# Attention's second product in two chains of 256 query columns instead of one of 512

## The chip, the core and the metric

The kernel runs on one core of one Trainium2 chip. The metric is the device time of one execution in microseconds (us). Before the change the median of three runs is 1011.43 us (1008.32 to 1012.51). TensorE multiplies matrices, VectorE (DVE) and ScalarE (ACT) work on tiles elementwise, GpSimd (POOL) does elementwise work on SBUF alone, and SyncE (SP) issues the DMAs of this kernel, one after the other from one queue.

## The reference

Four batches (B = 4) of 12288 queries with C = 128 channels attend to 768 pooled keys each; keys and values are the same matrix. What comes out goes through a gated convolution of five taps along the sequence.

```python
kv_pool = kv.reshape(B, H // r, r, W // r, r, C).mean(axis=(2, 4))   # r = 4
k = v = kv_pool.reshape(B, -1, C) @ w_sr                             # 768 x 128
s = (q @ k.transpose(0, 2, 1)) / np.sqrt(C)
a = np.exp(s - s.max(-1, keepdims=True))
a /= a.sum(-1, keepdims=True) + 1e-09
x = a @ v                                                            # "AV"
gate = sigmoid(sum(conv_w[k] * xp[:, k:k + S] for k in range(5)))    # xp: x, 4 zeros ahead
return (gate * (x @ w_val)) @ w_out
```

## The kernel before, in words

**Groups and tiles.** Queries are taken in groups of 512 (GQ), 24 per batch, 96 in all. A group has four tiles of 128 queries (NT = 4). Everything is kept with the channels or the queries on the partitions, and the output is transposed back on the host.

**A tile.** `score` (L335) makes the 128 × 768 scores in PSUM with six f32r matmuls of 384 columns: queries and keys are each split into a high and a low part, and three of the four products are summed. `row_max` (L349, DVE) takes the negated maximum, `expo` (L354, ACT) the exponential in place with its sum `z`, `norm` (L359, DVE) the reciprocal `r`. `p_hi` (L373, ACT) writes the normalized probabilities as f16 into `hl`, and `p_lo` (L376, DVE) what f16 left over into the other half of the same `hl` tile. One `hl` tile holds two tiles of queries (0 and 1, or 2 and 3 of a group), high and low. When the second of the two is done, `p_lo` issues one DMA transposition from SP (L383), which writes the pair, now with the keys on the partitions, into its half of the group's `pt` tile. `hl` has four buffers and so has `pt`; ACT may write an `hl` buffer again once its transposition has landed.

**AV.** `av_range` (L389) multiplies the values with `pt`. The 768 keys are six chunks of 128 (NCH = 6); for each chunk there are three products (high values × high probabilities, low × high, high × low), listed in `AV_ORDER`, 18 in all. Each is a weight load of 128 × 128 f16 values and a matmul over the 512 query columns of the group, and all 18 are summed in one PSUM tile `av`, which has one buffer. `av_slice` (L395) issues a stretch of the 18.

**The gated part.** `g_x` (L406, ACT) takes `av` out of PSUM into `x`. POOL makes the convolution of two groups at a time out of eight instructions of 1024 columns (`conv_step`, L428). ACT takes the tanh of it, `g_val` (L467) multiplies `x` with `w_val` on TensorE, `g_h` (L471, DVE) joins the two, `g_out` (L478) multiplies with `w_out`, and `g_evac` (L488, ACT) writes the output tile. Four groups are stored with one DMA.

**The order of the work.** Nothing schedules: the order is written by hand. The loop of L583 goes over all 384 tiles, `t`. In step `t` the scores of tile `t + 1` are issued first, then (for the tile before) `p_lo` with its DMA, a load of queries for four groups if it is due, `expo` of tile `t`, then a part of an older group's AV, then the rest. With a lag of one step, `mj` = 0, 1, 2, 3 counts the steps of a group, and `AV_CUTS` gives the parts of the AV of the group two back: at `mj` = 0 the products 0 to 2, at 1 the products 3 to 8 in two halves (something else may stand between them), at 2 the products 9 to 11, at 3 the products 12 to 17. At `mj` = 0, `g_out` of an older group stands on TensorE between the scores and AV; at `mj` = 2, `g_val` stands behind AV. The setup of the next batch's keys (loads of `kv` tiles at 8 of 24 groups until the last batch is loaded, sums on DVE, projections and transposes on TensorE) is spread over the steps.

**SP's queue** holds, in the order of the program: the transpositions, two per group; a load of queries and a store of output per four groups; the `kv` loads. 

**The end.** The last groups' gated parts are written out from L666. The last-but-one group's 18 products stand there in one piece (L681); the last group's AV is already made in two chains of 256 columns, in two banks (L702 to L706). Temporaries of these groups come from the pool `work`, under the names `th2` (two buffers) and `hh` (one).

Of the kernel before, what the change touches and what calls it, by code (L numbers as in the profile page):

```python
# [6 lines left out]
F32 = mybir.dt.float32  # L7
# [8 lines left out]
R = 4  # L16
P = 128
GQ = 512
NT = GQ // P
# [8 lines left out]
def attn_moe_kernel(ctx, tc, qT, kvT, w_sr, w_moe, outT):  # L28
# [3 lines left out]
    B, C, N = qT.shape  # L32
    PC = kvT.shape[4] // R
    NK, RR = PIECES * PC, R * R
    NCH = NK // P
# [2 lines left out]
    NW = w_moe.shape[1]  # L38
    TAPS = NW - 2 * C
    HALO = TAPS - 1  # L40
    AV_CUTS = (0, 3, 9, 12, 18)
    assert 3 * NCH == AV_CUTS[-1]
    scale = 1.0 / float(C) ** 0.5

    const = ctx.enter_context(tc.tile_pool(name="const", bufs=1))
    kvp = ctx.enter_context(tc.tile_pool(name="kvp", bufs=3))
    keys = ctx.enter_context(tc.tile_pool(name="keys", bufs=2))
    io = ctx.enter_context(tc.tile_pool(name="io", bufs=2))
    hlp = ctx.enter_context(tc.tile_pool(name="hlp", bufs=4))
    ptp = ctx.enter_context(tc.tile_pool(name="ptp", bufs=4))  # L50
    work = ctx.enter_context(tc.tile_pool(name="work", bufs=2))
    xp = ctx.enter_context(tc.tile_pool(name="xp", bufs=3))
# [6 lines left out]
    def misc():  # L59
        return ps_m.tile([P, GQ], F32, name="m")  # L60
# [248 lines left out]
    def quad_tile(g):  # L309
        g.quad = io.tile([C, 4, GQ], F32, name="q")  # L310
        for k in range(4):
            at(g.i + k).q = g.quad[:, k]

    def load_q(g, c0=0, c1=4 * GQ):
        nc.sync.dma_start(out=g.quad.rearrange("c i x -> c (i x)")[:, c0:c1],
                          in_=qT[g.b, :, g.t0 + c0:g.t0 + c1])
# [18 lines left out]
    def score(g, j, early=False):  # L335
        sl = slice(j * P, (j + 1) * P)
        kh, kl = g.st["kh"], g.st["kl"]
        s = bank_pair()
        passes = ((g.qh, kh), (g.qh, kl), (g.ql, kh))
        order = [(i, h) for i in range(3) for h in range(2)]  # L340
        if early:
            order.sort(key=lambda p: p[1])
        for i, h in order:
            a, k = passes[i]
            nc.tensor.matmul(s[:, h, :HALF], a[:, sl], k[:, h * HALF:(h + 1) * HALF],  # L345
                             start=(i == 0), stop=(i == 2))
        g.s[j] = s[:, :, :HALF]
# [6 lines left out]
    def expo(g, j):  # L354
        g.z[j] = small.tile([P, 1], F32, name="z")
        nc.scalar.activation(out=g.s[j], in_=g.s[j], func=AF.Exp, bias=g.nm.pop(j),  # L356
                             accum_out=g.z[j])
# [18 lines left out]
    def p_lo(g, j):  # L376

        nc.vector.scalar_tensor_tensor(out=part(g, j, 1), in0=g.s.pop(j), scalar=g.r.pop(j),  # L378
                                       in1=part(g, j, 0), op0=ALU.mult, op1=ALU.subtract)
        if j % 2:  # L380
            if g.pt is None:
                g.pt = ptp.tile([P, NT, 2 * NCH, P], F16, name="pt")
            nc.sync.dma_start_transpose(  # L383
                out=g.pt[:, j - 1:j + 1].rearrange("p j k q -> p (j k) q"),
                in_=g.hl.rearrange("p j a k -> p (j a k)"))

    AV_ORDER = [(v, k, a) for k in range(NCH) for v, a in (("vh", 0), ("vl", 0), ("vh", 1))]

    def av_range(g, out, lo, hi, j0=0, j1=NT):  # L389
        for i in range(lo, hi):  # L390
            v, k, a = AV_ORDER[i]
            nc.tensor.matmul(out, g.st[v][:, k * P:(k + 1) * P], g.pt[:, j0:j1, a * NCH + k],  # L392
                             start=(i == 0), stop=(i == len(AV_ORDER) - 1))

    def av_slice(g, lo, hi):  # L395
        if lo == 0:
            g.av = ps_av.tile([C, GQ], F32, name="av")
        av_range(g, g.av, lo, hi)

    def new_x(g):  # L400
        if g.i % 2 == 0:
            g.two = xp.tile([C, HALO + 2 * GQ], F32, name="x")
            at(g.i + 1).two = g.two
        g.x = g.two[:, g.i % 2 * GQ:g.i % 2 * GQ + HALO + GQ]

    def g_x(g, av, c0=0, c1=GQ):  # L406
        nc.scalar.activation(out=g.x[:, HALO + c0:HALO + c1], in_=av, func=AF.Copy,  # L407
                             scale=g.st["down"])
# [62 lines left out]
    def g_h(th, m, name="h", h=None):  # L471
        if h is None:
            h = work.tile([C, GQ], F32, name=name, bufs=2 if name == "h" else 1)
        nc.vector.scalar_tensor_tensor(out=h, in0=th, scalar=1.0, in1=m,  # L474
                                       op0=ALU.add, op1=ALU.mult)
        return h

    def g_out(h, m):  # L478
        nc.tensor.matmul(m, wout, h, start=True, stop=True)  # L479
        return m  # L480
# [22 lines left out]
    for b in range(B):  # L503
        for i in range(NG):
            g = Group()
# [6 lines left out]
    def at(i):  # L512
        return groups[i] if 0 <= i < G else None
# [31 lines left out]
    for n, i in enumerate(order):  # L545
# [3 lines left out]
        h = 2 * n // PIECES  # L549
# [3 lines left out]
        if n in ends:  # L553
            project(st, h, m, c0 - h * HALF, (n + 1) * PC - h * HALF)
            c0 = (n + 1) * PC
# [22 lines left out]
    def drip():  # L578
        if trickle:
            trickle.pop(0)()  # L580

    row_max(at(0), 0)
    for t in range(NT * G + LAG):  # L583
        gi, j = divmod(t, NT)
        cur, prev, nxt = (at(u // NT) for u in (t, t - 1, t + 1))
        load = j == 0 and gi % 4 == 0 and at(gi + 4)
        gi, mj = divmod(t - LAG, NT)
        avg, xg, vg, og = (at(gi - d) for d in (2, 3, 6, 7))
        cg = at(gi - 4 - gi % 2)

        if nxt:
            score(nxt, (j + 1) % NT)
        if og and mj == 0:
            og.m = g_out(og.h, misc())
        if prev and t <= NT * G:
            p_lo(prev, (j - 1) % NT)
        if load:
            quad_tile(load)
            load_q(load)
        if cur:  # L600
            expo(cur, j)
        if xg and mj == 0:
            new_x(xg)
            g_x(xg, xg.av)
        if og and mj == 1:
            out_tile(og)
            g_evac(og, og.m)
        evac = None
        if avg:
            av_slice(avg, AV_CUTS[mj], AV_CUTS[mj] + 3)  # L610
        if gi == 1 and mj > 0:
            evac = values(st, mj - 1)
        elif mj == 1 and gi > 0:
            evac = setup_product(gi)
        if avg:
            av_slice(avg, AV_CUTS[mj] + 3, AV_CUTS[mj + 1])
        if vg and mj == 2:
            vg.m = g_val(vg, misc())
            vg.th = g_tanh(vg.gate)
        if cg:  # L620
            if mj == 0 and cg.i == gi - 4:
                halo(cg, at(cg.i - 2), nc.gpsimd)
            conv_step(cg, gi % 2 * 4 + mj)
        if mj == 3 and gi >= 0 and at(gi + 2):
            g_qh(at(gi + 2))
        if t == 0:
            row_max(cur, 1)
        if cur:
            norm(cur, j)
            p_hi(cur, j)  # L630
        if nxt and t:
            row_max(nxt, (j + 1) % NT)
        if evac:
            evac()
        if mj == 1 and gi in highs:
            b, q = highs[gi]
            keys_high(states[b], q)
        if vg and mj == 3:
            vg.h = g_h(vg.th, vg.m)
        if gi >= 0 and mj < 3:  # L640
            setup_vector(gi, mj)
        if mj == 1 and gi in loads:
            b, p = loads[gi]
            load_kv(b, states[b], 2 * p)
        if (gi, mj) in halved:
            presum(states[1], halved[gi, mj])
        if gi < 3 and (gi, mj) > (1, 1) and (gi, mj) < (2, 1):
            n = 4 * gi + mj - 6
            values_high(st, n)
            values_low(st, n)  # L650
        if mj == 3 and gi in highs:
            b, q = highs[gi]
            keys_low(states[b], q)
        if mj == 3 and gi > 1 and gi % NG in (NG - 1, 0, 1) and (gi + 1) // NG < B:
            for f in (values_high, values_low):
                f(states[(gi + 1) // NG], (gi + 1) % NG)
        for _ in range(6 if t == 0 else 1):
            drip()
        if mj == 3 and gi >= 0 and at(gi + 2):
            g_ql(at(gi + 2))  # L660
        if mj == 3 and gi in scales:
            scale_values(states[scales[gi]], 0)
        if og and mj == 2 and og.i % 4 == 3:
            store_last(og, 4)

    n1, n2, n3, n4, n5, n6, n7 = groups[:-8:-1]  # L666
    half = GQ // 2
    two = lambda: (lambda p: (p[:, 0], p[:, 1]))(bank_pair())
    one = lambda: bank_pair()[:, 0]

    def gate_tile(name):
        return work.tile([C, GQ], F32, name=name)

    def av_bank():
        return ps_av.tile([C, GQ], F32, name="av")
# [2 lines left out]
    g_x(n3, n3.av)  # L678
    a0, a1 = two()
    n6.m, n5.m = g_val(n6, a0), g_val(n5, a1)  # L680
    av_slice(n2, 0, 18)  # L681
    n6.th, n5.th = g_tanh(n6.gate), g_tanh(n5.gate, gate_tile("th2"))
    halo(n4, n6, nc.scalar)
    acc4 = one()
# [1 line left out]
    n7.m = g_out(n7.h, misc())  # L686
    gate3 = conv_pool(n3)
    n6.h = g_h(n6.th, n6.m)
    n5.h = g_h(n5.th, n5.m, "hh")
    conv_rest(n4, acc4)  # L690
    new_x(n2)
    g_x(n2, n2.av)
# [30 lines left out]
    n2.m = g_val(n2, misc())  # L723
    n1.m = g_val(n1, one())
    n4.m = g_out(n4.h, n4.m)
    n3.h = g_h(n3.th, n3.m, "hh")
    n1.th = gate_tile("th2")
    for c in (0, half):
        g_tanh(acc1[:, c:c + half], n1.th[:, c:c + half])
# [2 lines left out]
    h = work.tile([C, 2 * GQ], F32, name="tap1", bufs=1)  # L732
# [40 lines left out]
```

## Time and profile before

| | |
|---|---|
| median of three runs | 1011.43 us |
| the profiled execution | 1011.84 us, its span 1010.0 us |
| TensorE clock granted | 0.996 of full speed |
| matmuls of AV (L392) in the profile | 1152 with the high values, 576 with the low ones |
| weight loads in the profile, all lines | 4523 |
| DMA transpositions | 192, from issue to landing 3.3 / 6.4 / 9.9 us (least, median, most) |

How to read it. The profile is of one execution. A row of the timeline is "start, duration, engine, line, operation, output <- inputs, shapes, count"; neighbouring equal instructions are joined. PE is TensorE's matmuls and PEld its weight loads, which run beside the matmuls; a matmul's recorded duration is its way through the array, and as matmuls overlap, what one costs is the step from its start to the next one's. "SPq" rows are instructions of SP's queue; their duration is the time for which SP was occupied by one. "idle <- X" or "A <- X: us, times, longest" is the idle time of an engine before an instruction, put down to what ended last; "issue" means that the profile shows nothing that was waited for. The chain is followed back from the last instruction, at each step to what released it.

### The profile page before, as it was taken

To read this page: it belongs to the slowest core of one execution; us is meant where nothing else is said; L and a number is where in the kernel's file an instruction comes from. 1 tells how busy PE (TensorE), PEld (TensorE's weight loads), DVE (VectorE), ACT (ScalarE), POOL (GpSimd) and SP (SyncE) were. 2 spreads that over 40 slices of the span, in tenths; PEclk is the share of its full clock that TensorE was granted. 3 is DMA by queue.
4 is the path that set the end of the run, shared out by engine and by line. 5 is a ranking of instruction groups with operands and counts; after the bars stand their busy time and mean duration, and the time that the engine had idled before them with its cause. 6 is when DMAs were issued, how large, how long until landed. Compare 5 with 4: busy or idle time off the path is not lost.

```text
span 1010.0 us, 14940 instructions
## 1 busy us (share of the span) xinstructions
PE 970.9 (96%) x4523; PEld 647.7 (64%) x4523; DVE 931.1 (92%) x1842; ACT 913.8 (90%) x1599; POOL 868.9 (86%) x653
## 2 busy tenths in 40 slices
PE   3789999999999999999999999999999999999998
PEld 3556666666666666666666666666666666666664
DVE  5899999999999999999999999999999999999996
ACT  1789999999999999989999999898999999999995
POOL 1659989888998889898899998889899989988993
PEclk9899999999999999999999999999999999999999
DMA  9799999999999999999999999999999999999995
GB/s 344 180 197 217 227 225 240 249 222 232 240 236 224 218 244 238 236 227 230 250 220 229 230 253 237 211 247 244 218 222 213 223 206 202 236 207 203 204 195 144
DMA packets 613087, 227.81 MB, mean 226 GB/s; under 512 B 597520, under 2 KB 598160, under 8 KB 607248
## 3 DMA queue, kind: packets, MB, share of 16 engines
q1 hardware_dynamic: 613008, 226.86, 107.2%
q8 instruction: 37, 0.61, 0.2%
q14 instruction: 42, 0.34, 0.1%
HBM read 50.66 MB, written 25.17 MB: 75 GB/s over the span
## 4 chain that ended last, share of the span: by engine, by line
PE 79%; DVE 6%; DMA 6%; ACT 2%; issue 1%; ACTq 0%; DVEq 0%
PE s L345 33%; PE av L392 32%; PE m L468 7%; PE m L479 6%; DMA pt<-hl 6%; DVE hl L378 3%; DVE nm L351 1%; ACT hl L374 1%; DVE h L474 1%; DVE s L447 0%; ACT s L356 0%; DVE r L365 0%; DVE pool L118 0%; PE m L210 0%; ACT o L489 0%
## 5 line engine op out<-in xcount | busy, mean ns | idle before, releaser
L426 POOL TENSOR_TENSOR acc<-acc,tap 128x1024 f32<-128x1024 f32 x184 | 437.2, 2376 | 7.2
L392 PE MATMUL av<-pt,vh 128*128 128x512 f16 (+1 forms) x1152 | 408.9, 380 | 12.1 <-DMA pt<-hl 5.2
L378 DVE SCALAR_TENSOR_TENSOR hl<-s,r,hl 128x768 f16<-128x768 f32 x384 | 388.8, 1012 | 25.5 <-ACT hl L374 21.5
L374 ACT ACTIVATE hl<-s,r 128x768 f16<-128x768 f32 x384 | 346.1, 901 | 45.7 <-DVE r L365 30.3
L351 DVE TENSOR_REDUCE nm<-s 128x1 f32<-128x768 f32 x384 | 362.8, 945 | 18.5 <-PE s L345 15.2
L356 ACT ACTIVATE s<-s,nm 128x768 f32<-128x768 f32 x384 | 335.5, 874 | 17.9 <-DVE nm L351 15.2
L345 PE MATMUL s<-kh,qh 128*128 128x384 f32 x768 | 288.2, 456 | 6.3 <-DVE z L363 5.6
L392 PEld LDWEIGHTS <-vh 128*128 128x128 f16 x1164 | 113.2, 97 | 171.1 <-issue 79.7
L392 PE MATMUL av<-pt,vl 128*128 128x512 f16 (+1 forms) x576 | 217.6, 378 | 0.0
L345 PEld LDWEIGHTS s<-kh,qh 128*128 128x128 f32 x768 | 145.7, 191 | 93.5 <-issue 47.3
L421 POOL TENSOR_SCALAR tap<-x,wm 128x1024 f32<-128x1024 f32 x184 | 204.5, 1126 | 0.0
L345 PE MATMUL s<-kh,ql 128*128 128x384 f32 x768 | 197.0, 337 | 0.0
L345 PE MATMUL s<-kl,qh 128*128 128x384 f32 x768 | 196.8, 337 | 0.0
L326 POOL TENSOR_TENSOR ql<-q,qh 128x512 fp32r<-128x512 f32 (+1 forms) x97 | 123.0, 1268 | 42.4 <-ACT qh L321 42.2
L345 PEld LDWEIGHTS s<-kl,qh 128*128 128x128 f32 x768 | 140.1, 189 | 0.0
L345 PEld LDWEIGHTS s<-kh,ql 128*128 128x128 f32 x768 | 139.7, 189 | 0.0
L421 POOL TENSOR_SCALAR acc<-x,wm 128x1024 f32<-128x1024 f32 x46 | 51.6, 1122 | 50.8 <-ACT x L407 50.2
L479 PE MATMUL m<-h,wm 128*128 128x512 f32 x182 | 93.0, 592 | 0.0
L468 PE MATMUL m<-x,wm 128*128 128x512 f32 x182 | 92.9, 592 | 0.0
L392 PEld LDWEIGHTS <-vl 128*128 128x128 f16 x582 | 57.5, 99 | 51.2 <-issue 29.8
L365 DVE RECIPROCAL r<-z 128x1 f32<-128x1 f32 x384 | 62.9, 164 | 13.1
L356 ACT ACTIVATION_READ_ACCUMULATOR s<-s,nm 128x1 f32 x384 | 74.6, 194 | 0.0
(84 smaller groups left out, 661.0 us busy)
## 6 DMA issues: line engine op xcount, KB each, us to landing
q<-in_q SPq DMA_DIRECT2D x23, 1024.0 KB, 6.0
out<-o SPq DMA_DIRECT2D x22, 1024.0 KB, 4.9
kvt<-in_kv SPq DMA_DIRECT2D x24, 768.0 KB, 5.3
pt<-in_kv SPq DMA_DIRECT2D x16, 384.0 KB, 7.9
pt<-hl SPq DMA_TRANSPOSE x192, 6.2
out<-o SPq DMA_DIRECT2D x3, 512.0 KB, 2.6
q<-in_q SPq DMA_DIRECT2D x1, 512.0 KB, 6.4
acc<-in_w_moe SPq DMA_DIRECT2D x1, 261.0 KB, 6.1
```

The lines of the kernel that those rows point to most:

```text
L326: nc.gpsimd.tensor_tensor(out=g.ql[:, c0:c1], in0=g.q[:, c0:c1], in1=g.qh[:, c0:c1].bitcast(F32), op=ALU.subtract)
L345: nc.tensor.matmul(s[:, h, :HALF], a[:, sl], k[:, h * HALF:(h + 1) * HALF], start=(i == 0), stop=(i == 2))
L351: nc.vector.tensor_reduce(out=nm, in_=g.s[j], axis=AX.XY, op=ALU.max, negate=True)
L356: nc.scalar.activation(out=g.s[j], in_=g.s[j], func=AF.Exp, bias=g.nm.pop(j), accum_out=g.z[j])
L365: nc.vector.reciprocal(out=g.r[j], in_=z)
L374: nc.scalar.activation(out=part(g, j, 0), in_=g.s[j], func=AF.Copy, scale=g.r[j])
L378: nc.vector.scalar_tensor_tensor(out=part(g, j, 1), in0=g.s.pop(j), scalar=g.r.pop(j), in1=part(g, j, 0), op0=ALU.mult, op1=ALU.subtract)
L392: nc.tensor.matmul(out, g.st[v][:, k * P:(k + 1) * P], g.pt[:, j0:j1, a * NCH + k], start=(i == 0), stop=(i == len(AV_ORDER) - 1))
L421: nc.gpsimd.tensor_scalar(out=t, in0=g.two[:, k:k + 2 * GQ], scalar1=cwt[:, k:k + 1], scalar2=1.0, op0=ALU.mult, op1=ALU.mult)
L426: nc.gpsimd.tensor_tensor(out=g.acc, in0=g.acc, in1=t, op=ALU.add)
L468: nc.tensor.matmul(m, wval, g.x[:, HALO + c0:HALO + c1], start=True, stop=True)
L479: nc.tensor.matmul(m, wout, h, start=True, stop=True)
```

## The change

The AV of a group becomes two chains of 18 products of 256 columns. The first sums over tiles 0 and 1 into the left half of the `av` tile, the second over tiles 2 and 3 into the right half. `AV_CUTS` is doubled, so that at `mj` = 0 and 1 the first chain is issued (6 and 12 products) and at `mj` = 2 and 3 the second (6 and 12). The pool of `hl` tiles has five buffers. To make room for it, `th2` and `hh` of the last groups are no longer taken from `work`: two of the `kv` buffers, which nothing loads any more at that point, are cut into six tiles of 512 columns (`spare`). Nothing else is different: the loop, the loads, the transpositions and the numbers of all other buffers stay.

```diff
-    AV_CUTS = (0, 3, 9, 12, 18)
-    assert 3 * NCH == AV_CUTS[-1]
+    AV_CUTS = (0, 6, 18, 24, 36)
+    assert 6 * NCH == AV_CUTS[-1]
...
-    hlp = ctx.enter_context(tc.tile_pool(name="hlp", bufs=4))
+    hlp = ctx.enter_context(tc.tile_pool(name="hlp", bufs=5))
...
     def av_slice(g, lo, hi):
+
         if lo == 0:
             g.av = ps_av.tile([C, GQ], F32, name="av")
-        av_range(g, g.av, lo, hi)
+        for n in range(2):
+            c0, n0 = n * GQ // 2, n * len(AV_ORDER)
+            av_range(g, g.av[:, c0:c0 + GQ // 2], max(lo - n0, 0), min(hi - n0, len(AV_ORDER)),
+                     n * NT // 2, (n + 1) * NT // 2)
...
         if avg:
-            av_slice(avg, AV_CUTS[mj], AV_CUTS[mj] + 3)
+            av_slice(avg, AV_CUTS[mj], AV_CUTS[mj] + 6)
...
         if avg:
-            av_slice(avg, AV_CUTS[mj] + 3, AV_CUTS[mj + 1])
+            av_slice(avg, AV_CUTS[mj] + 6, AV_CUTS[mj + 1])
...
+    idle = [kvp.tile([C, 2, R, PC * R], F32, name="kvt").rearrange("c n r x -> c (n r x)")
+            for _ in range(2)]
+    spare = [t[:, c:c + GQ] for t in idle for c in range(0, 3 * GQ, GQ)]
+
     def gate_tile(name):
-        return work.tile([C, GQ], F32, name=name)
+        return spare.pop() if name == "th2" else work.tile([C, GQ], F32, name=name)
...
-    av_slice(n2, 0, 18)
+    av_slice(n2, 0, AV_CUTS[-1])
...
-    n5.h = g_h(n5.th, n5.m, "hh")
+    n5.h = g_h(n5.th, n5.m, h=spare.pop())
...
-    n3.h = g_h(n3.th, n3.m, "hh")
+    n3.h = g_h(n3.th, n3.m, h=spare.pop())
```

## The prediction

> **What bounds the kernel now.** I read the page first, for the busy shares and the chain that ended last.
>
> ```profile
> PE 970.9 (96%) x4523; PEld 647.7 (64%) x4523; DVE 931.1 (92%) x1842; ACT 913.8 (90%) x1599; POOL 868.9 (86%) x653
> PE 79%; DVE 6%; DMA 6%; ACT 2%; issue 1%; ACTq 0%; DVEq 0%
> ```
>
> TensorE is busy nearly all the time and holds 79% of the chain; the transpositions (DMA pt<-hl) hold 6%. Where the two meet is seen by stage, in the busy times of three stretches:
>
> ```profile
> core 0: us, PE busy (x) PEld busy (x) DVE busy (x) ACT busy (x) POOL busy (x), PEclk, DMA share, GB/s
> 100.00:230.00 130.00, 130.00 (x612) 86.95 (x611) 125.73 (x256) 124.05 (x217) 117.74 (x86) 1.00 1.12 231
> 230.00:690.00 460.00, 452.04 (x2115) 300.05 (x2112) 434.56 (x879) 428.92 (x747) 415.73 (x306) 1.00 1.12 234
> 690.00:980.00 290.00, 290.00 (x1363) 193.91 (x1362) 267.48 (x512) 275.40 (x476) 262.84 (x189) 1.00 1.06 213
> ```
>
> From 100 to 230 us and from 690 to 980 us TensorE never idles. All its idle time in the steady part, 460 − 452 = 8.0 us, lies between 230 and 690 us. The answer on the AV line says for what it waited there (us, times):
>
> ```profile
>   DMA pt<-hl: 8.8, 11
> ```
>
> So eleven times the weight load in front of a group's AV waited for a transposition, 8.8 us in all. Two of the waits show on the chain, each with the transposition from its issue to its landing:
>
> ```profile
> 445.21 5.71 DMA pt<-hl
> 450.91 0.14 issue
> ...
> 675.24 9.43 DMA pt<-hl
> 684.67 0.14 issue
> 684.81 0.81 PE av L392 x3
> ```
>
> In both cases AV starts 0.14 us after the landing. What a group costs where nothing waits is read from the chain at 800 us, from one product with wm to the next of its kind:
>
> ```profile
> 798.81 0.86 PE m L468 x2
> 799.66 1.04 PE s L345 x6
> 800.71 1.31 PE av L392 x6
> ...
> 803.92 0.65 PE av L392 x3
> ...
> 807.98 0.66 PE av L392 x3
> 808.64 0.86 PE m L468 x2
> ```
>
> 808.64 − 798.81 = 9.83 us for a group. The group's first AV slice is at 803.92 and its third at 807.98, 4.06 us later.
>
> Why the transpositions are late is a matter of SP's queue. Near the last wait (first the DVE instruction that completes a tile pair, then SP):
>
> ```profile
> 674.42 1.01 DVE L378 SCALAR_TENSOR_TENSOR hl<-s,r,hl 128x768 f16<-128x768 f32 x1
> ...
> 680.76 0.53 SPq L315 DMA_DIRECT2D q<-in_q  x1
> 681.40 6.44 SPq L383 DMA_TRANSPOSE pt<-hl  x1
> ...
> 834.01 1.02 DVE L378 SCALAR_TENSOR_TENSOR hl<-s,r,hl 128x768 f16<-128x768 f32 x1 [0.17 <-ACT hl L374]
> ...
> 835.10 5.44 SPq L383 DMA_TRANSPOSE pt<-hl  x1
> ```
>
> The pair finished at 675.43 is issued only at 681.40, 6.0 us late; at 835 us, where no kv tiles are loaded any more, the delay is 0.07 us. And SP has no gap at the end of the loaded stretch:
>
> ```profile
> 681.40 21.77 SPq L383 DMA_TRANSPOSE pt<-hl  x5
> 703.27 0.53 SPq L495 DMA_DIRECT2D out<-o  x1
> 703.89 14.08 SPq L383 DMA_TRANSPOSE pt<-hl  x3
> 718.07 0.53 SPq L315 DMA_DIRECT2D q<-in_q  x1
> 718.70 21.30 SPq L383 DMA_TRANSPOSE pt<-hl  x5
> ```
>
> Each row begins where the one before it ends. So in that stretch the waits of TensorE have a second cause behind them: a queue that serves as fast as it can.
>
> **The change part by part.** The sum is made against the profiled execution's own 1011.84 us (span 1010.0 and 1.84 around it), 0.41 above the median of 1011.43.
>
> *Two chains of 256 columns.* The trace has both forms, at its end:
>
> ```profile
> 988.28 0.38 PE L392 MATMUL av<-pt,vh 128*128 128x512 f16 x1
> ...
> 991.95 0.38 PE L392 MATMUL av<-pt,vh 128*128 128x512 f16 x1
> ...
> 994.74 0.27 PE L392 MATMUL av<-pt,vh 128*128 128x256 f16 x1
> ...
> 998.56 0.27 PE L392 MATMUL m<-pt,vh 128*128 128x256 f16 x1
> 998.67 0.59 PE L468 MATMUL s<-x,wm 128*128 128x512 f32 x1
> ```
>
> From the first to the last of 18 wide ones are 17 steps in 3.67 us, 0.2159 each; from the first to the last of 36 narrow ones 35 steps in 3.82 us, 0.1091 each. Per group 36 × 0.1091 − 18 × 0.2159 = 3.928 − 3.886 = 0.042 us more. TensorE sets the pace from about 100 to 980 us, 880 / 9.83 = 89 groups: +3.7 us. The bounds: 0, if a narrow one took exactly half; +6.6 us, if it took the 0.110 that an 18-step chain of 1.98 us gives (36 × 0.110 − 3.886 = 0.074 per group). I take 3.7, since it is the same instruction, merely elsewhere.
>
> [...]
>
> *36 more weight loads per group.* Their rows, and those of the scores:
>
> ```profile
> L392 PEld LDWEIGHTS <-vh 128*128 128x128 f16 x1164 | 113.2, 97 | 171.1 <-issue 79.7 <-DMA pt<-hl 3.6
> L345 PEld LDWEIGHTS s<-kh,qh 128*128 128x128 f32 x768 | 145.7, 191 | 93.5 <-issue 47.3 <-PE s L345 2.9 <-DVE z L363 1.6
> ```
>
> An f16 load of 97 ns fits beside a matmul of 109 ns, which the 0.1091 already shows. The f32 load that follows a chain has 191 ns in the record and now only 109 ns of cover instead of 216. The one place where the trace has this, 998.56 to 998.67, has the f32 product starting 0.11 us after the last narrow one: nothing is left uncovered. I take 0; the other end is 0.191 − 0.109 = 0.082 us, four times a group, +29 us (a rival below).
>
> *The second half is asked for 4.06 us later.* The order of TensorE's queue at the start of one group's AV; the names behind "waits" are counters, DMAHW those of transfers. Before:
>
> ```order
> L479 MATMUL m<-h,wm 128x512 [waits DVE_49]
> L392 LDWEIGHTS vh [waits DMAHW5_49,DMAHW3_49]
> L392 MATMUL av<-pt,vh 128x512 [waits Activation_49]
> L392 LDWEIGHTS vl
> L392 MATMUL av<-pt,vl 128x512
> ```
>
> Now, the first chain and, some 40 rows on, the start of the second:
>
> ```order
> L483 MATMUL m<-h,wm 128x512 [waits DVE_49]
> L392 LDWEIGHTS vh [waits DMAHW0_49]
> L392 MATMUL av<-pt,vh 128x256 [waits Activation_49]
> ...
> L345 MATMUL s<-kh,ql 128x384
> L392 LDWEIGHTS vh
> L392 MATMUL av<-pt,vh 128x256 [waits DMAHW2_49]
> L392 LDWEIGHTS vl
> ```
>
> The first load waits for one transposition instead of two, and the wait for the pair of tiles 2 and 3 has moved behind two score tiles. Behind the moved wait stand that chain and the next scores, for which DVE and ACT wait. The old waits, by the view of who waited for whom (us, times, longest):
>
> ```profile
> PE av L392 <- DMA pt<-hl: 5.2, 7, 1.6
> PEld L392 <- DMA pt<-hl: 3.6, 4, 1.6
> ```
>
> None is over 1.6 us, so 4.06 covers each of them taken alone: −8.8 us.
>
> *The fifth hl buffer.* ACT waited for the transposition of an old pair:
>
> ```profile
> ACT hl L374 <- DMA pt<-hl: 2.1, 3, 1.1
> ```
>
> With the queue allowed to run later this would grow; a fifth buffer gives one pair, 4.9 us, more. I count 0 on the path: the waits fell where TensorE waited too.
>
> *The tail.* DVE, ACT and SP keep their order, the temporaries only take other memory, and the 36 narrow matmuls there cost 0.04 us. 0.
>
> **The sum, by two accounts.** By TensorE's: 1011.84 − 8.8 + 3.7 = 1006.7. But the queue has an account of its own. Its services don't get shorter, and while it never runs empty it can't land a pair sooner. The first pair of the last late group was issued at 681.40, and the answer on that one transposition and the load that begins the group's AV read:
>
> ```profile
> DMA to landing us min/median/max: 8.5/8.5/8.5
> ...
> 694.21 0.10 PEld L392 LDWEIGHTS <-vh 128*128 128x128 f16 x1 [0.24 <-issue]
> ```
>
> It lands at 689.9, and with the 0.14 us seen above AV can start at 690.0 instead of 694.21: 4.2 us sooner and no more, however few the waits. Where the queue begins to lag, somewhere between 100 us and the first idle time after 230, TensorE comes up to 13 groups × 0.042 = 0.5 us later than before; I take 0.2: 4.0. After that TensorE is alone again and pays 0.042 on (980 − 694) / 9.83 = 29 groups, +1.2. So 1011.84 − 4.0 + 1.2 = 1009.0, and 0.41 less on the scale of the median: 1008.6. The account that comes out later holds. What stays of the waits is about 2 us around 680 us, now for a first pair behind a load of q.
>
> **The rivals.**
> - *Nothing is held back by the queue* (it serves faster when left to run ahead, so TensorE's account holds): 1006.7 − 0.4 = 1006.3. For it: the waits were for the second pair, the first had 4 us to spare. Against it: the rows without a gap. 0.14.
> - *Slower, by the f32 weight loads:* if only 109 of 191 ns are covered, the first score product after each chain slice starts 0.082 us later, +29 us: about 1037. It decides from 0.02 us per change of type on (7 us). Against it stands the start after 0.11 us. 0.06.
> - *Slower, by the pace at which instructions reach TensorE:* a group has 92 loads and matmuls in 9.83 us now (107 ns each) and 128 then; it decides from 9.87 / 128 = 77 ns. The densest steady rows are the scores, 12 in 1.04 us, 87 ns; at that pace 72 of AV take 6.26 us, 2.3 more a group, +207 us. The narrow chains ran at 0.1091 / 2 = 55 ns over 72, so I give it 0.04. [...]
> - *The change does not free what it should:* the wait only changes its place, to the first pair or to a late second chain, which holds up scores, DVE and ACT. No gain, the price stays: up to 1011.4 + 3.7 = 1015. For it: first pairs behind q loads have the least to spare. 0.10.
>
> **How the numbers follow.** The forecast has the rest, 0.66, with 1006.6 to 1010.8 of its own (the three runs before spread over 4.2 us). A measurement of this kernel tells about 0.5%, 5 us, from no change: 1006.4 and 1016.5 are the limits. Faster by more: half of the first rival and the edge of the forecast, 0.12. Slower by more: the two slower rivals and a part of the last, 0.13. Within: 0.75. The range 1005.5 to 1013.5 leaves out the slow rivals, half of the last and the fast edge, some 0.2.
>
> **What would show it.** Right: the AV line's wait for transpositions falls from 8.8 to some 2 us and lies near 680 us; narrow matmuls follow each other at 0.109; a group takes 9.87 at 800 us; SP's rows stay without a gap from 300 to 700 us. Wrong: a group of over 9.95 us at 800 us (weight loads or issue), or AV of the group above starting well before 690 us (the queue was not the limit), or a sum of waits as before at the second chain.

## The result, and the profile after

The changed kernel takes 1016.40 us in the median of five runs (1014.54 to 1019.17), the kernel before, in five runs on the same chip, 1010.07 us (1008.32 to 1012.51). The ratio is 1.0067 (95% interval 1.0044 to 1.0090): slower by 0.4 to 0.9%. The forecast was 1008.6 us with a range to 1013.5, so the time lies above the range. The profiled execution took 1018.22 us (span 1016.4), 6.4 us more than the 1011.84 of before.

The page's busy times and the shares of the chain that ended last, and the number of instruction fetches from its section on DMA queues (packets, MB, share of 16 engines):

```profile
PE 976.8 (96%) x6233; PEld 786.8 (77%) x6233; DVE 932.4 (92%) x1842; ACT 914.6 (90%) x1599; POOL 868.9 (85%) x653
...
q8 instruction: 49, 0.80, 0.3%
...
PE 82%; DMA 8%; DVE 5%; ACT 4%; issue 1%; SPq 0%; ACTq 0%
```

The transpositions' share of the chain went up, from 6% to 8%. Queue q8 is one of two of the kind "instruction", 0.80 MB / 49 = 16 KB a fetch. On the page of before it has this row:

```profile
q8 instruction: 37, 0.61, 0.2%
```

Its fetches go with the rows of TensorE in the trace, waits included: 9526 before and 12664 after, 257 and 258 to a fetch, while VectorE has 2043 and 2042, ScalarE 2004 and 2014, and GpSimd 823 and SyncE 544 in both. So q8 is taken here for TensorE's instruction stream.

The busy times by stage, in the three stretches of the prediction:

```profile
100.00:230.00 130.00, 130.00 (x841) 105.16 (x840) 124.80 (x253) 123.05 (x214) 116.73 (x85) 1.00 1.13 225
230.00:690.00 460.00, 452.67 (x2921) 365.18 (x2920) 432.55 (x877) 427.31 (x746) 413.16 (x306) 1.00 1.13 232
690.00:980.00 290.00, 288.68 (x1869) 233.47 (x1867) 266.02 (x507) 273.22 (x470) 260.23 (x186) 1.00 1.10 215
```

TensorE is idle for 460 − 452.67 = 7.3 us in the middle stretch, where it was 8.0, and now for 1.3 us more after 690 us. What the AV line waited for (us, times), and two of these waits in the timelines of weight loads and of matmuls (start, duration, the idle time in brackets):

```profile
  DMA pt<-hl: 15.5, 16
```

```profile
697.65 0.10 PEld L392 LDWEIGHTS <-vh 128*128 128x128 f16 x1 [1.05 <-DMA pt<-hl]
```

```profile
703.01 0.27 PE L392 MATMUL av<-pt,vh 128*128 128x256 f16 x1 [1.10 <-DMA pt<-hl]
```

The first row begins the AV of group 64, the one of which the prediction spoke: it waits for its first pair of tiles, which was never late before (in the groups from 300 to 700 us it had landed 2.8 us or more before AV began). The second row is the head of its second chain, 5.36 us later, and it waits again. By the single rows of the trace seven groups wait at the first load and six at the head of the second chain, up to 2.0 us. Of the 8.6 us for which the matmuls are idle from 230 to 980 us, 5.8 lie at the heads of second chains and 2.8 at first loads. (A wait of a load and of its own matmul are counted apart in the 15.5, so the two sums of before and after aren't compared; the idle time by stage is.) So the waits changed their place and did not get less.

What a group costs, from the chain at 800 us:

```profile
803.85 0.86 PE m L472 x2
804.71 1.07 PE s L345 x6
805.78 1.32 PE av L392 x12
...
813.75 0.86 PE m L472 x2
```

813.75 − 803.85 = 9.90 us, 0.07 more than the 9.83 of before; 9.87 was foretold. And the queue of SP, by the rows of its 23rd and its 129th transposition, first of the kernel before, then of the changed one:

```profile
142.13 3.66 SPq L383 DMA_TRANSPOSE pt<-hl  x1
...
681.40 6.44 SPq L383 DMA_TRANSPOSE pt<-hl  x1
```

```profile
142.85 4.39 SPq L383 DMA_TRANSPOSE pt<-hl  x1
...
689.48 6.03 SPq L383 DMA_TRANSPOSE pt<-hl  x1
```

The 129th is the first pair of group 64. For the same 106 transpositions and 46 other transfers between these two rows the queue took 539.3 us before and takes 546.6 us now. In both kernels it is never idle there: between one row and the next lie some 0.1 us, 14.7 us in all in either kernel, and two of these gaps alone are over 0.3 us. So the queue works 7.3 us longer on the same work.

Where? The single rows of the trace show it. A transposition that directly follows another and meets no fetch occupies SP for 3.67 us (mean of 40 before; 3.68, 37, after). One that meets a fetch of q8 alone takes 4.32 (8) before and 4.27 (14) after. Two neighbours in the changed kernel:

```profile
575.50 3.62 SPq L383 DMA_TRANSPOSE pt<-hl  x1
...
579.21 4.39 SPq L383 DMA_TRANSPOSE pt<-hl  x1
```

And the DMA view of these two stretches (busy share of the 16 DMA engines in 40 slices, in tenths; the time of a packet, one piece of a transfer, is put down to the slice in which it starts), the first without a fetch, the second with one:

```profile
DMA  9999999999999799999999999999999999999999
```

```profile
DMA  9999999999889999999000010001008999999999
...
q8 instruction: 1, 0.02, 1.3%
```

For eleven slices of 0.11 us, 1.2 us, the DMA engines stand nearly still while the transposition is under way. The fetch starts at 580.81 us and takes about 1 us; the standstill begins half a microsecond after its start. By the single packets it is no accident of this pair: all 8 such transpositions before and 12 of the 14 after that meet a fetch of q8 alone have 0.9 to 1.6 us in which fewer than 10 packets start per 0.1 us, where some 85 are usual, and one packet in them lasts 1.1 to 1.7 us; of the 40 and 37 without a fetch none has over 0.4 us of it. Behind the standstill shown, some 113 packets start per 0.1 us, so part of the lost time is made up.

### The profile page after: what moved, and what is told of

Read it like the earlier page. It is cut to its first block, busy times and chain, and to the rows that moved or that the text cites. A ratio compares the mean times of both kernels' runs of the same rounds, so it can differ in the third digit from the quotient of the medians.

```text
span 1016.4 us, 18087 instructions
## 1 busy us (share of the span) xinstructions
PE 976.8 (96%) x6233; PEld 786.8 (77%) x6233; DVE 932.4 (92%) x1842; ACT 914.6 (90%) x1599; POOL 868.9 (85%) x653
## 4 chain that ended last, share of the span: by engine, by line
PE 82%; DMA 8%; DVE 5%; ACT 4%; issue 1%; SPq 0%; ACTq 0%
PE s L345 33%; PE av L392 32%; DMA pt<-hl 7%; PE m L472 7%; PE m L483 7%; DVE hl L378 3%; ACT hl L374 2%; DVE nm L351 1%; DMA pt<-in_kv 1%; ACT s L356 1%; DVE pool L118 1%; PE s L141 0%; PE m L562 0%; PE m L210 0%; PE s L472 0%
## 5 line engine op out<-in xcount | busy, mean ns | idle before, releaser
L392 PE MATMUL av<-pt,vh 128*128 128x256 f16 x2292 | 443.2, 274 | 12.8 <-DMA pt<-hl 7.9
L392 PE MATMUL av<-pt,vl 128*128 128x256 f16 x1146 | 312.3, 273 | 0.0
L392 PEld LDWEIGHTS <-vh 128*128 128x128 f16 x2304 | 224.7, 98 | 94.9 <-issue 65.9
L345 PE MATMUL s<-kh,qh 128*128 128x384 f32 x768 | 258.7, 418 | 6.2 <-DVE z L363 5.6
L345 PEld LDWEIGHTS s<-kh,qh 128*128 128x128 f32 x768 | 123.9, 192 | 55.3 <-issue 45.9
L392 PEld LDWEIGHTS <-vl 128*128 128x128 f16 x1152 | 113.3, 98 | 49.0 <-issue 39.4
```

## The experiments

Four accounts are told apart. A: more TensorE instructions mean more fetches of its instruction stream, and each holds up the queue. B: the fifth buffer or the changed places in memory do it. C: the doubled weight loads do it by reading the same memory. D: the queue is late only because TensorE is. Times are medians with the ratio to the kernel before on the same chip and its 95% interval.

### e1: the buffers alone

The changed kernel with `AV_CUTS` and the lines of AV as before:

```diff
-        for n in range(2):
-            ...
+        av_range(g, g.av, lo, hi)
```

> The fifth buffer for high and low halves and the changed places of the temporaries at the end, with the one wide chain of before. Theory A (more TensorE instructions mean more fetches of the instruction stream, and each fetch holds up the queue of transpositions): 37 fetches as before, the 129th transposition issued within 1.5 us of the 681.40 us of before, AV waits of 7 to 10 us in all, time within 2 us of before. Rival B (the buffer or the changed places in memory slow the transpositions): the 129th transposition near 689 us, time 4 to 7 us over before.

1010.65 us, ratio 0.9999 (0.9981 to 1.0018), 37 fetches, 129th transposition at 681.65. The waits by who waited (us, times, longest):

```profile
PE av L392 <- DMA pt<-hl: 5.6, 10, 0.9
PEld L392 <- DMA pt<-hl: 4.3, 7, 1.5
```

As A expected. B falls, and the prediction's zeros for the buffer and for the end of the program hold.

### e2 and e9: fillers instead of chains

The kernel before with instructions that do nothing:

```diff
-        av_range(g, g.av, lo, hi)
+        for i in range(lo, hi):
+            av_range(g, g.av, i, i + 1)
+            for _ in range(2):
+                nc.tensor.sem_inc(spin, 1)
```

In e2 the increments stand in `av_range`, so the end of the program has them too.

> The kernel before, with two semaphore increments behind each wide AV product on TensorE's queue (36 a group, on a semaphore that nobody waits for): as many more instructions as in the changed kernel, but no more matmuls and weight loads. Theory A (fetches): 49 to 51 fetches instead of 37, the 129th transposition issued 6 to 10 us after the 681.40 us of before, the AV waits of before grow, time 4 to 8 us over before; a group at 800 us stays at 9.83 us. Rival C (the doubled weight loads slow the transpositions by reading the same memory) and rival D (the queue is only late because TensorE is): about 50 fetches, but the 129th transposition within 1.5 us of 681.40, time within 2 us of before, unless the fillers themselves hold TensorE up, which a group of over 9.85 us at 800 us would show.

1026.42 us, 1.0161 (1.0141 to 1.0181), 51 fetches. The 129th transposition is at 685.67 us, 4.3 us late and so less than expected, but the 23rd came earlier too (140.51): between the two the queue took 545.2 us, 5.9 more than before. At the end the fillers held TensorE up:

```profile
1007.94 0.37 PE L393 MATMUL m<-pt,vl 128*128 128x256 f16 x1
1008.24 0.70 PE L393 MATMUL m<-pt,vh 128*128 128x256 f16 x2
```

0.30 us a step instead of 0.109. Without these:

> e2 again without the fillers in the 36 narrow products that end the program, where they held TensorE up (steps of 0.30 us instead of 0.109, 7 us in all). Kernel before, wide chains, 36 more instructions a group that do nothing. Theory A (a queue that is never idle, and that each further fetch of instructions makes later): 50 or 51 fetches, the 129th transposition 4 to 8 us after 681.40, AV of group 64 about as much after 694.21, and 0.04 us a group on top after that: 1015 to 1019 us, so the same loss as the changed kernel's without one narrow matmul. Rival D (only what TensorE itself takes longer counts, 0.04 us a group as e2 showed at 800 us): 3.5 us over before at most, about 1014, and the 129th transposition no later than TensorE is.

1022.23 us, 1.0113 (1.0087 to 1.0139): above what A expected. 50 fetches; the rows of the 23rd and the 129th transposition:

```profile
139.26 3.67 SPq L384 DMA_TRANSPOSE pt<-hl  x1
```

```profile
685.79 5.85 SPq L384 DMA_TRANSPOSE pt<-hl  x1
```

546.5 us between them, as in the changed kernel, with no matmul and no weight load more than before. That speaks for A and against C. The rows of before and after speak against C and D too: where no fetch is met, a transposition takes 3.67 and 3.68 us, though TensorE loads twice as many AV weights in the second (3456 loads for 1746), and the gaps of the queue are the same 14.7 us, so it doesn't wait for TensorE. The time of e9 could not be used yet, since it was not known what the fillers themselves cost; e15 measures it.

### e3 to e6: AV two tile steps later

```diff
-        avg, xg, vg, og = (at(gi - d) for d in (2, 3, 6, 7))
+        vg, og = (at(gi - d) for d in (6, 7))
+        ai, aj = divmod(t - LAG - 2, NT)
+        avg, xg = (at(ai - d) for d in (2, 3))
...
-            av_slice(avg, AV_CUTS[mj], AV_CUTS[mj] + 3)
+            av_slice(avg, AV_CUTS[aj], AV_CUTS[aj] + 3)
```

`x` and the convolution follow `aj` in the same way, and half of one group's AV moves into the end of the program. e4 is the same on the changed kernel.

> One wide chain and five buffers as in e1, but a group's AV, its x and its convolution come two tile steps (4.9 us) later: both pairs of tiles get the room that the change gave only to the second, with no instruction more. Theory A: 37 fetches, the 129th transposition within 1.5 us of 681.40, AV waits under 1 us, a group of 9.83 us at 800 us, time 4 to 8 us under before (8.8 us of waits less, up to 4 us back at the end of the program, where half a group of AV is added). Rival B or a queue that follows TensorE (it gets later whenever it is allowed to): the waits stay above 5 us and the time is within 2 us of before.

> The changed kernel (two narrow chains, five buffers) with AV two tile steps later as in e3: what the narrow chains cost where nothing waits for a transposition. Theory A: 49 fetches, the 129th transposition 6 to 10 us after 681.40, AV waits under 2 us all the same, a group of 9.90 us at 800 us, time e3 plus 89 groups by 0.07, so 5 to 7 us over e3. Rival (the price of the narrow chains is the 0.042 us a group that their steps show): 3 to 4.5 us over e3. Rival D: the 129th transposition within 1.5 us of that of e3 plus what TensorE is later there.

1052.70 us, 1.0425 (1.0404 to 1.0445), and 1055.02 us, 1.0444 (1.0424 to 1.0464): both miss by far. No instruction of AV waits for a transposition any more, but another wait took the place. The costliest group of TensorE in e3 (busy, mean ns | idle before):

```profile
L392 PE MATMUL av<-pt,vh 128*128 128x512 f16 (+1 forms) x1152 | 407.4, 379 | 40.2 <-ACT x L408 40.2
```

AV has one PSUM bank. Two steps later the next group's AV comes one score tile after the end of the last, and ACT has not yet read the bank out. e5 and e6 put the products with wval in between:

```diff
+        if vg and mj == 2:
+            vg.m = g_val(vg, misc())
         if avg:
             av_slice(avg, AV_CUTS[aj], AV_CUTS[aj] + 3)
...
         if vg and mj == 2:
-            vg.m = g_val(vg, misc())
             vg.th = g_tanh(vg.gate)
```

> e3 with one thing mended: there AV's single bank was not yet read out when the next group's AV came 1.04 us (one score tile) after the end of the last (40.2 us of waits for x on ACT). Now the two products with wval (0.86 us), which stood behind AV in that tile step, stand ahead of it, so that 1.9 us lie between, as in the kernel before. Theory A: no wait for transpositions, none over 3 us in all for x, a group of 9.83 us at 800 us, 37 fetches; time 4 to 8 us under before (8.8 us of waits less, up to 4 us back at the end of the program). Rival: ACT, which now has x and tanh in one tile step, is late for the scores, and a group stays over 9.95 us at 800 us: over 1020 us.

> The changed kernel with the order of e5: two narrow chains where nothing waits for a transposition. If the narrow chains cost 0.07 us a group on TensorE: e5 plus 5 to 7.5 us. If they cost the 0.042 us of the prediction: e5 plus 3 to 4.5 us. Fetches 49, and still no wait for transpositions over 1 us in all.

1028.33 us, 1.0168 (1.0150 to 1.0185), and 1026.41 us, 1.0154 (1.0136 to 1.0172). The rival of e5 came true: a group takes 10.02 us, and DVE waits for ACT.

```profile
L378 DVE SCALAR_TENSOR_TENSOR hl<-s,r,hl 128x768 f16<-128x768 f32 x384 | 388.8, 1012 | 64.3 <-ACT hl L374 63.6
```

Here ACT and DVE set the pace, so the narrow chains cost nothing that can be seen (e6 against e5), and the pair says nothing of their price.

### e7 and e8: without the kv loads

```diff
-        t = kvp.tile([C, 2, R, PC * R], F32, name="kvt")
-        nc.sync.dma_start(out=t, in_=kvT[b, i:i + 2].rearrange("n c r x -> c n r x"))
+        if len(once) < 2:
+            t = kvp.tile([C, 2, R, PC * R], F32, name="kvt")
+            nc.sync.dma_start(out=t, in_=kvT[b, i:i + 2].rearrange("n c r x -> c n r x"))
+            once.append(t)
+        t = once[i // 2 % 2]
```

> The kernel before, which loads only the first two kv tiles of the second batch and uses these two again in place of the 24 loads of batches 1 to 3 (their keys and values are then others; all work on the engines stays). The queue of transpositions gets 24 transfers of 768 KB less. Theory A: the waits of AV for transpositions go (under 1 us), a group at 500 us takes 9.83 us as at 800 us, and the time is 7 to 10 us under before: that is all that the change could have gained. Rival (the waits of 230 to 690 us have another cause than the queue): waits over 5 us, time within 3 us of before.

> The changed kernel without those 24 loads, as in e7 (other keys and values for batches 1 to 3): the price of the narrow chains by itself, since neither kernel waits for transpositions. If TensorE pays 0.07 us a group over some 89 groups: e7 plus 5 to 7.5 us. If it pays the 0.042 us of the prediction: e7 plus 3 to 4.5 us. If the loss came from the queue alone: e7 plus less than 2 us. Fetches 49 in any case.

1000.17 us, 0.9891 (0.9874 to 0.9909), and 1007.07 us, 0.9957 (0.9941 to 0.9974). In neither does AV wait for a transposition. The middle stretch of both, e7 first:

```profile
230.00:690.00 460.00, 459.79 (x2157) 307.15 (x2156) 442.16 (x897) 437.23 (x763) 422.79 (x312) 1.00 1.04 211
```

```profile
230.00:690.00 460.00, 459.81 (x2973) 371.69 (x2971) 439.94 (x893) 434.85 (x759) 420.14 (x311) 1.00 1.07 211
```

TensorE is busy throughout. So the price of the narrow chains by themselves is 1007.07 − 1000.17 = 6.9 us (6.7 by the ratios), not 3.7. And the loads cost the kernel before 1 − 0.9891 = 1.1%, some 11 us, which is all that the change could have gained; they cost the changed kernel 1.0067 − 0.9957 = 1.1%, the same. The change freed nothing.

### e10: the chains with four buffers

The kernel before with the changed `AV_CUTS` and `av_slice`, `hl` and the end as before.

> The changed kernel with four buffers for high and low halves, as before, and the old places at the end: the two chains alone. Theory A: 49 fetches, the same price; the queue runs up to 12 us late in the changed kernel, 6 us with four buffers' room before, so ACT waits for a free buffer more often: 0 to 5 us over the changed kernel. Rival B (the fifth buffer is what costs): 4 to 7 us under the changed kernel.

1017.75 us, 1.0073 (1.0045 to 1.0101), 49 fetches, 547.0 us between the two transpositions. Within A's expectation, and B is out for good. TensorE hardly waits for transpositions here (0.7 us); ACT does, for a free buffer:

```profile
ACT hl L374 <- DMA pt<-hl: 19.1, 19, 2.2
```

So the queue's lateness shows at TensorE with five buffers (15.5 us of waits in the changed kernel) and at ACT with four (19.1 us).

### e11 and e12: AV later without more instructions

e11 cuts AV anew (with an empty first slice), on e1:

```diff
-    AV_CUTS = (0, 3, 9, 12, 18)
+    AV_CUTS = (0, 0, 7, 11, 18)
```

> One wide chain, five buffers, and AV's 18 products cut 0, 7, 4 and 7 over the four tile steps instead of 3, 6, 3 and 6: AV starts 1.05 us later, for both pairs, with no instruction more. If the queue sets the end of the loaded stretch (it can't land a pair sooner, so a later start gains its own delay once): AV waits 1 us less in all and the time 0.5 to 2 us under before. If each wait counts by itself (none over 1.6 us): the AV waits fall from 8.8 to about 1 us and the time is 6 to 8 us under before. Rival: two score tiles in a row hold TensorE up for want of a free bank: a group of over 9.85 us at 800 us and a time over before.

1012.43 us, 1.0012 (0.9992 to 1.0032). The waits did fall:

```profile
PE av L392 <- DMA pt<-hl: 2.9, 2, 1.6
```

But the new cut has its own price: 9.85 us a group, and 10.49 instead of 10.15 in every sixth group, where a projection of the next batch's keys falls. Gain and price cancel; the run doesn't tell the two accounts of a wait apart.

e12 takes e5 and gives each tile step of ACT one long instruction again:

```diff
-        if vg and mj == 2:
+        if vg and mj == 3:
             vg.th = g_tanh(vg.gate)
...
-        if mj == 3 and gi >= 0 and at(gi + 2):
+        if (mj == 3 if gi < 1 else mj == 0) and gi >= 0 and at(gi + 2):
             g_qh(at(gi + 2))
...
-        if mj == 3 and gi >= 0 and at(gi + 2):
+        if mj == (1 if gi > 0 else 3) and gi >= 0 and at(gi + 2):
             g_ql(at(gi + 2))
```

> e5 (one wide chain, five buffers, AV and what hangs on it two tile steps later) with ACT's work spread again as before, one long instruction a tile step: tanh goes one tile step later, the high half of q two steps earlier than in the kernel before and its low half to the step in which POOL has no convolution. In e5 a group took 10.02 us at 800 us and DVE waited 64 us for ACT. Theory A: 9.83 us a group at 800 us, no wait for a transposition, 37 fetches; time 4 to 8 us under before. Rival: some other engine's order still holds the scores up: over 9.9 us a group, and then 6 us or more over before.

1006.58 us (twelve runs, 1004.51 to 1010.41), 0.9965 (0.9948 to 0.9982): faster than the kernel before by 0.2 to 0.5%, and the fastest of all that do the whole work. A group takes 9.81 us, there are 37 fetches, and of the waits is left:

```profile
PE av L392 <- DMA pt<-hl: 3.3, 4, 1.6
```

So what the change was after is to be had, for both pairs, by a later AV in one wide chain. The waits did not vanish, although that was expected, and the gain is at the lower end of the expectation (4.1 us by the medians, 3.5 by the ratio).

### e13 and e14: five half loads

```diff
+        n = 1 if (b, i) in ((1, 12), (2, 4), (2, 12), (3, 4), (3, 12)) else 2
-        nc.sync.dma_start(out=t, in_=kvT[b, i:i + 2].rearrange("n c r x -> c n r x"))
+        nc.sync.dma_start(out=t[:, :n], in_=kvT[b, i:i + n].rearrange("n c r x -> c n r x"))
         for k in range(2):
-            st["kv", i + k] = t[:, k]
+            st["kv", i + k] = t[:, min(k, n - 1)]
```

> The changed kernel with 5 of its 24 kv loads cut to half (384 KB; the second piece of keys is then made from the same rows as the first). A whole load costs the queue some 2.5 to 3 us, so this gives it about 7 us back, as much as the 12 fetches take. If the queue's time counts one for one: the 129th transposition 6 to 9 us earlier than the changed kernel's 689.48, AV waits at 4 to 9 us instead of 15.5, and the time 4 to 8 us under the changed kernel. If only TensorE's own price counts: under 2 us.

> The kernel before with the same five half loads. If the queue's time counts one for one: 4 to 8 us under before, not below the 1000.2 us of the kernel without any of the loads; AV waits at 0 to 3 us instead of 8.8. If not: within 2 us of before.

The changed kernel takes 1009.58 us, 0.9998 (0.9983 to 1.0013), which is 0.7% or 7 us under the 1.0067 without the edit. The kernel before takes 1005.02 us, 0.9950 (0.9936 to 0.9965), 5 us less. Between the two transpositions the queue took 533.2 us in e14, 6.1 less than before, and 543.1 us in the one profiled execution of e13, which at 1011.8 us is among its slower ones, 3.5 less than the changed kernel. The waits of e13 and of e14:

```profile
PEld L393 <- DMA pt<-hl: 5.1, 8, 1.6
PE av L393 <- DMA pt<-hl: 5.0, 7, 1.2
```

```profile
PEld L393 <- DMA pt<-hl: 2.5, 4, 1.4
PE av L393 <- DMA pt<-hl: 1.4, 4, 0.4
```

10.1 and 3.9 us, each a little above what was expected; the 129th transposition of e13 is at 683.20, within the expectation. But the main thing is answered: in both the 129th transposition comes 6.3 us earlier (675.13 for 681.40 in e14, 683.20 for 689.48 in e13), and the kernels are 5 and 7 us faster. Time given to the queue comes back in the time of the kernel about one for one; it follows that time which fetches take from it is lost in the same way, though no run takes the fetches alone away.

### e15: what the fillers cost by themselves

e7 with the fillers of e9.

> e7 (before, without the 24 kv loads) with the fillers of e9: what 36 semaphore increments a group cost TensorE where nothing waits for a transposition. By the group of 9.87 instead of 9.83 us at 800 us: e7 plus 3 to 5 us; what e9 lost beyond that (11.6 us in all over before) is then the queue's, some 7 us. If the fillers themselves cost 9 us or more here, e9 says nothing about the queue's part in the time.

1009.33 us, 0.9985 (0.9973 to 0.9997): 9.2 us over e7 (9.5 by the ratios), so they cost TensorE much more than one group at 800 us showed. By its own expectation, then, the time of e9 says little of the queue's part; what stands of e9 is its queue, 546.5 us. The loads cost 1.0113 − 0.9985 = 1.3% there.

## Why the prediction was wrong, point by point

**What bounds the kernel: right.** TensorE's own work and, from 230 to 690 us, a queue without a gap. Without the loads (e7) TensorE has no gap either.

**A narrow step of 0.109 us: right.** The median of the narrow steps in the changed kernel's loop is 0.109 as well. **The weight loads of the scores: right at 0**; no 29 us came, nor the 207 us of a slow instruction pace.

**The price of 3.7 us: mis-sized.** It measured 6.9 us (e8 against e7), 0.07 us for each group at 800 us where 0.042 was summed. The 0.042 is in it. The other 0.03 lies outside the chains, in the products that follow one. A score tile in the timeline of before and after, from its first product to the first of AV:

```profile
799.10 0.91 PE L345 MATMUL s<-kh,qh 128*128 128x384 f32 x2
...
800.55 0.39 PE L392 MATMUL av<-pt,vh 128*128 128x512 f16 x1
```

```profile
804.15 0.92 PE L345 MATMUL s<-kh,qh 128*128 128x384 f32 x2
...
805.62 0.28 PE L392 MATMUL av<-pt,vh 128*128 128x256 f16 x1
```

1.45 us and 1.47. Over all tiles of e7 and e8 between 100 and 980 us the steps behind the first take 173.3 to 174.2 ns on average before and 174.1 to 175.2 after, 3.6 ns more a tile; four tiles a group make some 0.015 of the 0.03, and the rest is spread over other products. Why they are slower was not tried. The bound of +6.6 us had the right size for a wrong reason.

**The removed waits, −8.8 by one account and −4.2 by the other: the step that failed.** It stands in the second account: "Its services don't get shorter, and while it never runs empty it can't land a pair sooner." Shorter they did not get, and the sum took them as unchanged. They got longer: 7.3 us between the two transpositions, because there are twelve more fetches of instructions (37 to 49), and a transposition that meets one takes 4.3 us instead of 3.67. TensorE's 12664 rows are 3138 more than the 9526 of before, 261 for each fetch more. The same shows with 50 and 51 fetches and no narrow chain (e2, e9), and not with 37 and five buffers (e1):

| | fetches | 23rd to 129th transposition, us |
|---|---|---|
| before | 37 | 539.3 |
| e1, buffers alone | 37 | 539.9 |
| e11, e12, AV later | 37 | 540.0, 540.5 |
| changed kernel | 49 | 546.6 |
| e10, chains with four buffers | 49 | 547.0 |
| e2, e9, fillers | 51, 50 | 545.2, 546.5 |

These are the kernels with all loads in which the queue has no gap between the two (in e3 to e6 it has some of over 0.5 us). No row with 37 is over 540.5 and none with more is under 545.2. By size: between the two transpositions 28 fetches fall instead of 21. At 4.32 − 3.67 = 0.65 us each these 7 are an estimated 4.6 us of the 5.4 by which the transpositions got longer; another 1.7 us are in the issues of two q loads, each of which meets a fetch.

The 8.8 us were a little too high besides: they count the wait at 389.84 us once for the load and once for its matmul (0.5 us), and the idle time of the stage was 8.0.

TensorE itself hardly shows the fetches (in e8, with 49 of them, it is idle for 0.2 of the 460 us of the middle stretch), but a transposition loses 0.65 us to each that it meets (0.59 in the changed kernel: 3.68 to 4.27).

**The account itself held.** With the queue as it was, AV of group 64 would have started at 690.0. Its transposition was issued 8.1 us later (681.40 to 689.48), so 698.1 is due, and the row has 697.65. Against 694.21 before that is 3.4 us of loss in place of 4.2 us of gain. After that TensorE pays 0.07 on for some 30 groups, 2.1 us, and the late second chain at 703.01 adds up to 1.1 of waiting: 6.6 us, near the 6.4 at the end. TensorE's own account, closed with what was measured, says the same in other words: 89 groups at 0.067 us are 6.0 us more work, and its idle time from 230 to 980 us went from 8.0 to 8.6. The price was paid in full, and the slower queue kept the idle time, which was to pay for it, as large as before. The account that comes out later holds, as the prediction said; its input was off by 8 us.

**The rivals.** The fourth came, "the change does not free what it should": the wait went to the first pair and to late second chains. It had 0.10 and its price was again 3.7, so it ended at 1015 instead of 1016.4. The sign that the prediction named, a sum of waits as before at the second chain, came for the larger part: from 230 to 980 us TensorE is idle for 8.6 us, a little over the 8.0 of before, and 5.8 of them lie at the heads of second chains. The mechanism that it lacked is the fetch.

**The fifth buffer at 0: right** (e1). What it changes is where the lateness shows: with four buffers it appears as 19.1 us of waits on ACT (e10), in about the same time (1.0073 against 1.0067).

What stays open: why the scores after a narrow chain are slower, and why a fetch brings nearly all packets of a transposition to a stop, for which the trace has the times alone; and what the changed kernel would take with 37 fetches, which no run has with narrow chains.

## What to carry to other kernels

Where a DMA queue without gaps sets the end of a stage, ask of each edit what it adds to the traffic on the DMA engines, the instruction stream too: the page's row of instruction fetches is to be read before and after. Here, cutting matmuls in half to relax a wait made that stream longer by a third (37 to 49 fetches), and what the later wait gained the queue lost again; the same room was had by issuing the consumer later in the old order (e12, 1006.58 us), with one long instruction a step kept for ACT (without that, in e5, a group took 10.02 us instead of 9.81). And a price taken from one chain of a profile left out what the neighbours paid (0.042 us a group for 0.07): a group's period was the surer measure.

## What the runs showed of the hardware

- A fetch of 16 KB of TensorE's instructions made a DMA transposition that was under way 0.65 us longer before (3.67 to 4.32 us, 8 cases) and 0.59 us after (3.68 to 4.27, 14 cases); in 20 of the 22 hardly a packet started on the DMA engines for 0.9 to 1.6 us, which none of 77 transpositions without a fetch shows. A fetch on the other instruction queue (q14, 8 KB) cost 0.2 to 0.3 us (3.94 instead of 3.67, 11 cases before; 3.86 instead of 3.68, 6 cases after).
- Two semaphore increments behind a weight load and a matmul of 0.109 us a pair made the step 0.30 us (e2), about 0.10 us for each. 36 a group, behind wide products, cost 9.2 us in all (e15).
